# Sigmoid attention with a two-layer product after it: another order of loads, of partial products and of VectorE's sums

## The chip, the cores and the metric

The kernel runs on one core of one Trainium2 chip. The metric is the device time of one execution in microseconds (us). All runs quoted were at a granted TensorE clock of 0.997 to 1.0 wherever the record lists it. A span is the time from the first to the last instruction of the one execution that was profiled; it is 1.7 to 1.8 us shorter than the time of the same run.

PE is TensorE, DVE is VectorE, ACT is ScalarE, POOL is GpSimd (which issues the loads here) and SP is SyncE.

## The reference

```python
# q, k, v: (8, 12, 448, 64)   w_in: (768, 2048)   w_out: (2048, 768)
scores = matmul(q, k^T) / sqrt(64) - log(448)
attn   = matmul(1 / (1 + exp(-scores)), v)
x      = attn.transpose(0, 2, 1, 3).reshape(3584, 768)
h      = x @ w_in
out    = (h * cos(h)) @ w_out
```

## The kernel before

The kernel is written by a small scheduler. It keeps a model clock, keeps lists of what could be done next on each engine, and emits one instruction group at a time. What comes out is a fixed program: each engine runs its own queue in order and waits where its next instruction is not ready. The parameters at the head of the kernel steer only that order.

PE has these kinds of work. "T": transposes of early q and k. "S": scores. "AV": the sigmoid of the scores times v. "m1": the first product, `x @ w_in`. A **block**: 256 rows of the second product. The first block is plain. Each of the other 13 is made by a scheme with seven partial products instead of eight. A partial product is eight matmuls into one PSUM bank (the memory that TensorE writes its sums to), and VectorE then drains the bank, that is, copies or adds its contents to where they are needed.

```python
ORDER = [1, 6, 2, 7, 5, 4, 3]              # the seven products, in PE's order

def pe_prod(i, p, bk):                     # eight 128x384 matmuls into bank bk
    lhs, rhs, first, last = {
        1: (a11, b11, True, False),  2: (a12, b21, False, True),
        3: (s4, b22, False, True),   4: (a22, t4, False, True),
        5: (s1, t1, True, False),    6: (s2, t2, True, False),
        7: (a21, b12, False, False),
    }[p]
    ...
def dve_prod(p, bk, st, p1):               # the drain of that bank
    o = banks[bk][:, 0:HD]
    if p == 1:   nc.vector.tensor_copy(out=p1, in_=o)
    elif p == 2: nc.vector.tensor_copy(out=stages[st[0]], in_=o)
    elif p == 6: tt(stages[st[1]], o, p1, ALU.add)
    ...                                    # 7, 4 alike; 5 and 3 add to a stage
def gsum(eng, i, n, m, parts): ...         # s1, s2, a21 - .., s4: four sums per block
def dve_g(b, fp, part, hslot, cslot): ...  # h * cos(h), in pieces of 64 to 384 rows

def try_dve():                             # what VectorE gets next
    i = min(range(len(dve_q)), key=lambda n: (dve_q[n][0], n))   # priority, then age
    if DVE_PICK.get(dve_n[0], -1) < len(dve_q):
        i = DVE_PICK.get(dve_n[0], i)                            # or a set place
    ...
def try_pe():                              # what PE gets next
    kind = PE_PICK.get(order_at[0])        # a set kind at a set decision,
    ...                                    # otherwise S, T, AV, blocks, m1 by rules
for tok in LOADS.split():                  # the order of the first loads
    add_load(tok)
```

Two banks serve the blocks: products 1 and 2 fill one in turn, 6, 7 and 4 the other, and 5 and 3 take the first again. So PE may start a product only when VectorE has drained the product before the last. Besides its drains and sums VectorE copies the first product out of PSUM ("hs"), multiplies h by its cosine (line L355), and prepares q and k for the transposing DMA ("ri", L236).

Of the kernel before, what the change touches and what calls it, by code (L numbers as in the profile page):

```python
# [12 lines left out]
def kernel(  # L13
# [42 lines left out]
    N_RI = 2  # L56
    SIN_BURST = 3
    SIN_MIN = 1
    SIN_AT = [33]
    N_SIG0 = 4  # L60
    AV_MIN0 = 1
    AV_MIN = 6
# [2 lines left out]
    S_MAX2 = 2  # L65
    K_PIECE = 2
    M1_OPEN = 2
    M2_AT = [18, 10, 25, 58, 44, 52, 13, 44, 56, 62, 49, 48, 58, 64]
    M2_EAGER = True
    LOADS = 'y2 q1 x1 v0 x0 q2 v1 v3 q3 y0 x3 v2 q4 x2 b3 v4 b0 y1 y3 q5 q6 o0 b1 v8 v5 q7 v7 o1 b2 o3 v6 o2 q8'  # L70
    N_PLAIN = 1
    P_G = 2
    P_W = 2
    P_AV = 0
    P_IL = 1
    DUP_DVE = 4
    DUP_LEAD = 1.2
    P_DUP = 1
    T_LATE = 4
    T_AHEAD = 18  # L80
    HALF1 = 6
    HALF3 = 8
    HALF_MAX = 4
    W_POOL = False
    W_PIECES = 4
    G_POOL = ()
    PE_PICK = {28: 'm', 57: 't', 75: 'm', 539: 'm', 604: 'm'}
    DVE_PICK = {79: 2, 154: 1}
    WARM = 9
    WARM_END = 90.0  # L90
    TP_LAND = 9.0
    RAW_MARGIN = 3.0
    OUT_LAND = 4.0
# [134 lines left out]
    def dve_T(s, i, bk, j0, j1):  # L228
        dst = (kTs, qTs)[i][s % N_QKT]
        src = banks[bk].bitcast(fp16)[:, 0 : 2 * S].rearrange("p (x t) -> p x t", x=2)  # L230
        nc.vector.tensor_copy(out=dst[:, :, PT * j0 : PT * j1], in_=src[:, :, PT * j0 : PT * j1])
# [62 lines left out]
    def dve_dup(s, y):  # L294
        x = xts[s % N_X]
        nc.vector.tensor_copy(
            out=x[64 - 64 * y : 128 - 64 * y, 1], in_=x[64 * y : 64 * y + 64, 0]
        )
# [93 lines left out]
    def dve_wsum(n):  # L392
        b11, b12, b21, b22 = w_quarters()
        t1, t2, t4 = w_sum
        if n == 0:
            tt(t1, b12, b11, ALU.subtract)
        elif n == 1:
            tt(t2, b22, t1, ALU.subtract)
        elif n == 2:
            tt(b12, b22, b12, ALU.subtract)  # L400
        else:
            tt(t4, b21, t2, ALU.subtract)
# [180 lines left out]
    def add_load(tok):  # L583
        n = int(tok[1:])
        seen.add(tok)
        loads.extend(
            {
                "q": lambda: l_kq(n),
                "v": lambda: l_v(n),
                "a": lambda: l_wi(n, 0, 2),  # L590
                "b": lambda: l_wi(n, 2, 3),
                "x": lambda: l_wi(n, 0, 1),
                "y": lambda: l_wi(n, 1, 2),
                "w": lambda: l_wi(n),
                "o": lambda: l_wo(n),
            }[tok[0]]()
        )

    for tok in LOADS.split():
        add_load(tok)  # L600
# [16 lines left out]
    def wsums():  # L617
# [3 lines left out]
        for n in range(4):  # L621
            dve_q.append((P_W, 1.67, lambda n=n: dve_wsum(n), fin))

# [76 lines left out]
    def m1_job():  # L700
# [10 lines left out]
        b, fp = m1_next  # L711
        if b >= B or len(m1_open) >= M1_OPEN or len(m1_half) >= HALF_MAX:
            return None
# [91 lines left out]
    def start_av(s, js):  # L805
# [12 lines left out]
        def done():  # L818
# [12 lines left out]
            def fin():  # L831
# [6 lines left out]
                if s < DUP_DVE or ahead < DUP_LEAD:  # L838
                    for y in range(2):
                        dve_q.append((min(pri, P_DUP), 0.3, lambda y=y: dve_dup(s, y), dup_fin))  # L840
                else:
# [14 lines left out]
    def t_job():  # L856
# [3 lines left out]
        if (  # L860
            s_next[0] >= NJ * s - T_AHEAD
            and raw_got.get(s, 0) > (i if s else t_next[0])
# [6 lines left out]
    def start_t(s, i, j0, j1):  # L869
# [5 lines left out]
        def done():  # L875
# [3 lines left out]
            def fin():  # L879
# [6 lines left out]
            dve_q.append(  # L886
                (-2 if s_next[0] < SIN_AT[0] else 1, 0.065 + 0.067 * n, lambda: dve_T(s, i, bk, j0, j1), fin)
            )
# [182 lines left out]
    def try_pe():  # L1071
        if busy["pe"]:
            return
        kind = PE_PICK.get(order_at[0])
        order_at[0] += 1
# [16 lines left out]
    def heuristic():  # L1092
# [18 lines left out]
        jobs = NFP * m1_next[0] + m1_next[1]  # L1111
        want = not m1_open and quad_i[0] < NQUAD and jobs >= M2_AT[quad_i[0]]
        if j2 is not None and (want or (M2_EAGER and not m1)):
# [13 lines left out]
    def warm_up():  # L1127
        if clock[0] < WARM_END and s_next[0] < NJ * NSU:
            cur = av_cur.get(av_next[0])
            if any_bank():  # L1130
                pe_warm((single_free or pair_free)[0], 0, 128, ident)
            elif cur:
                pe_warm(cur["wd"], S, 512 - S, ident)
            else:
                return
            mode[0] = "full"
            run("pe", 0.055 if any_bank() else 0.03, lambda: None, 0.0)
# [35 lines left out]
    def try_act():  # L1173
# [12 lines left out]
        if not m2_on and len(hs_ready) >= SIN_BURST:  # L1186
            late = True
        if bursts[0] < len(SIN_AT) and sig_n[0] < SIN_AT[bursts[0]] and (act_q or hs_free or hs_extra) and table[0] == "sig":
            b_ok = False
# [37 lines left out]
    def try_dve():  # L1227
        if busy["dve"] or not dve_q:
            return
        i = min(range(len(dve_q)), key=lambda n: (dve_q[n][0], n))  # L1230
        if DVE_PICK.get(dve_n[0], -1) < len(dve_q):
            i = DVE_PICK.get(dve_n[0], i)
        dve_n[0] += 1
# [87 lines left out]
```

## Time and profile before

| | before |
|---|---|
| time, median of 4 runs | 382.24 us (380.77 to 382.8) |
| span of the profiled run | 379.6 us |
| PE, DVE, ACT busy | 97%, 77%, 69% |
| first 128x384 matmul | 83.0 us |
| last matmul ends | 375.3 us |

PE's busy time tells little here, because records of matmuls overlap. I use another measure throughout: the **time that PE lost** up to a moment. It is that moment less the sum of PE's useful work before it at its undisturbed pace: 0.189 us for a set of four 64x64 tiles of 448 columns, 0.1625 us for a 128x384 matmul, 0.0275 us for a transpose; small warm-up matmuls count as loss. These paces are the median distances between starts in undisturbed stretches of the trace before.

Of the profile before, the prediction below shows the tail. Here is the middle: the order of time in block 3, which took 10.4 us instead of 9.1. Columns: start, length, engine, line, operation, and in brackets how long the engine had idled and what ended that.

```profile
169.69 0.40 DVE L236 COPY ri<-qraw 128x896 f16<-128x896 f16 x1 [0.30 <-DMA qraw<-in_q_dram]
170.00 0.55 DVE L456 COPY p<-bk 128x384 f32<-128x384 f32 x1
170.47 1.15 DVE L355 TENSOR_TENSOR g_ring<-hs,cs 128x128 f16<-128x128 f32 x2
170.61 3.00 PE L426 MATMUL bk<-wo,g_ring 128*128 128x384 f16 x16 [0.43 <-DVE p L456]
171.54 0.55 DVE L365 TENSOR_TENSOR stage<-bk,p 128x384 f32<-128x384 f32 x1
172.00 1.15 DVE L355 TENSOR_TENSOR g_ring<-hs,cs 128x128 f16<-128x128 f32 x2
173.07 0.55 DVE L458 COPY stage<-bk 128x384 f32<-128x384 f32 x1
```

VectorE's queue is in order. A preparation that waited 0.30 us for a DMA stood ahead of the first drain (170.00), and PE, which needed that bank, started its third product 0.59 us late. After that come two cosine products (1.07 us) and a drain (0.47 us) for each product of PE. That is 1.54 us where PE needs 1.30.

### The profile page before, as it was taken

How to read it: one execution, taken by the hardware profiler on the slowest of the kernel's cores; microseconds unless marked ns; L12 is line 12 of the kernel's file. 1: busy time of each engine (PE TensorE's matmuls, PEld its weight loads, DVE VectorE, ACT ScalarE, POOL GpSimd, SP SyncE). 2: the span in 40 equal slices, each digit the busy share in tenths (PEclk: the TensorE clock that was granted, in tenths of full speed). 3: DMA queues.
4: the chain of work that ended last, by engine and by line, in shares of the span. 5: the costliest groups of instructions: out<-in, count | busy, mean ns of one | idle time of the engine just before them, and what ended most of it. 6: DMA issues, size and time to landing. Idle time of an engine off the chain costs nothing.

```text
span 379.6 us, 12680 instructions
## 1 busy us (share of the span) xinstructions
PE 369.2 (97%) x5563; PEld 232.7 (61%) x5563; DVE 292.9 (77%) x494; ACT 260.7 (69%) x266; POOL 69.5 (18%) x105
## 2 busy tenths in 40 slices
PE   8999999999999999999999999999999999999995
PEld 5666576665675775665665765565666566555553
DVE  2387889979999769569679597848586999868662
ACT  4989899996988896798796966574999744111000
POOL 8669531220311220220220202020000000000000
PEclk9999999999999999999999999999999999999999
DMA  9999999999999699599698947396411210133333
GB/s 160 201 197 199 203 212 206 149 130 130 119 161 127 136 121 161 86 157 123 95 157 155 114 83 127 77 120 150 82 26 26 54 35 2 32 71 67 85 83 83
DMA packets 70278, 44.60 MB, mean 117 GB/s; under 512 B 32592, under 2 KB 70224, under 8 KB 70224
## 3 DMA queue, kind: packets, MB, share of 16 engines
q0 software_dynamic: 30000, 22.49, 45.7%
q1 hardware_dynamic: 40144, 21.22, 31.6%
q8 instruction: 43, 0.70, 0.8%
q14 instruction: 11, 0.09, 0.1%
q10 hardware_dynamic: 80, 0.10, 0.1%
HBM read 45.61 MB, written 11.01 MB: 149 GB/s over the span
## 4 chain that ended last, share of the span: by engine, by line
PE 36%; DVE 11%; ACT 4%; issue 2%; DVEq 0%; ACTq 0%
PE bk L426 17%; PE pr L316 7%; PE bk L316 6%; DVE g_ring L355 5%; PE pr L277 3%; PE pr L251 3%; DVE hs L330 2%; ACT sig L260 2%; DVE stage L365 2%; ACT cs L333 1%; ACT L333 1%; DVE gs L390 1%; DVE g_ring L390 1%; DVE stage L458 0%; DVE xt L287 0%
## 5 line engine op out<-in xcount | busy, mean ns | idle before, releaser
L260 ACT ACTIVATE sig<-pr,lgs_t 128x896 f16<-128x896 f32 x159 | 148.6, 1011 | 41.1 <-PE pr L251 40.7
L316 PEld LDWEIGHTS <-wi 64*64 64x64 f16 x3072 | 99.7, 107 | 45.7 <-issue 3.2
L316 PE MATMUL pr<-xt,wi 64*64 64x448 f16 x2000 | 111.1, 349 | 0.4 <-DVE xt L287 0.2
L333 ACT ACTIVATE cs<-hs,pih_t 128x896 f16<-128x896 f32 x62 | 60.8, 1033 | 30.1 <-DVE hs L330 29.2
L355 DVE TENSOR_TENSOR g_ring<-hs,cs 128x768 f16<-128x768 f32 (+2 forms) x132 | 72.9, 589 | 1.4 <-ACT cs L333 1.1
L316 PE MATMUL bk<-xt,wi 64*64 64x448 f16 x1072 | 63.8, 349 | 0.3 <-DVE hs L330 0.2
L251 PE MATMUL pr<-qT,kT 64*64 64x448 f16 x672 | 61.0, 355 | 1.9 <-ACT sig L260 1.7
L426 PEld LDWEIGHTS <-g_ring 128*128 128x128 f16 x416 | 39.7, 98 | 33.1 <-issue 8.3
L330 DVE COPY hs<-pr 128x896 f32<-128x896 f32 x41 | 44.5, 1087 | 18.5 <-PE pr L316 16.2
L426 PE MATMUL bk<-wo,g_ring 128*128 128x384 f16 x312 | 55.7, 326 | 1.7 <-DVE stage L365 1.1
L184 POOL DMA_DIRECT2D vt<-in_v_dram x21 | 14.8, 706 | 178.7 <-PE pr L277 157.6
L426 PEld LDWEIGHTS <-gs 128*128 128x128 f16 x312 | 30.5, 98 | 21.1 <-issue 1.0
L426 PE MATMUL bk<-ws,gs 128*128 128x384 f16 x208 | 38.0, 326 | 0.1
L251 PEld LDWEIGHTS <-kT 64*64 64x64 f16 x672 | 26.1, 105 | 18.3 <-issue 6.8
L330 DVE COPY hs<-bk 128x448 f32<-128x448 f32 x42 | 24.2, 616 | 11.8 <-PE bk L316 11.6
L287 DVE CAST xt<-pr 128x896 f16<-128x896 f32 x19 | 20.7, 1089 | 14.5 <-PE pr L277 14.5
L277 PE MATMUL pr<-sig,vt 64*64 64x448 f16 x504 | 31.1, 350 | 0.0
L365 DVE TENSOR_TENSOR stage<-bk,p 128x384 f32<-128x384 f32 x39 | 21.6, 553 | 8.4 <-PE bk L426 8.4
L277 PEld LDWEIGHTS <-vt 64*64 64x64 f16 x588 | 18.9, 107 | 9.1 <-issue 1.3
L333 ACT ACT_TABLE_LOAD x16 | 20.5, 1283 | 5.1 <-DVE hs L330 4.8
L260 ACT ACT_TABLE_LOAD x15 | 19.2, 1283 | 5.7 <-PE pr L251 5.4
L426 PE MATMUL bk<-wo,gs 128*128 128x384 f16 x104 | 19.0, 326 | 0.3 <-DVE stage L365 0.2
(72 smaller groups left out, 285.3 us busy)
## 6 DMA issues: line engine op xcount, KB each, us to landing
out_dram<-stage SPq DMA_DIRECT2D x111, 96.0 KB, 2.2
vt<-in_v_dram POOLq DMA_DIRECT2D x21, 224.0 KB, 5.2
kraw<-in_k_dram POOLq DMA_DIRECT2D x19, 224.0 KB, 5.7
qraw<-in_q_dram POOLq DMA_DIRECT2D x19, 224.0 KB, 6.8
wi<-in_moe_w_in_dram POOLq DMA_DIRECT2D x24, 128.0 KB, 6.4
wo<-in_moe_w_out_dram POOLq DMA_DIRECT2D x4, 768.0 KB, 13.4
xt<-xt SPq DMA_DIRECT2D x24, 112.0 KB, 5.7
ws<-in_k_dram POOLq DMA_DIRECT2D x4, 224.0 KB, 7.4
```

What stands on the lines that cost most here:

```text
L184: nc.gpsimd.dma_start(out=vt_of(s), in_=v[b, 4 * g : 4 * g + 4].rearrange("(y x) (p j) d -> (x p) y (j d)", y=2, j=NJ),)
L251: nc.tensor.matmul(out=pairs[wd][64 * x : 64 * x + 64, y, 0:S], lhsT=kT[64 * y : 64 * y + 64, x, PT * j : PT * j + PT], rhs=qT[64 * y : 64 ...
L260: nc.scalar.activation(out=sgs[slot], in_=pairs[wd][:, :, 0:S], func=AF.Sigmoid, bias=lgs_t, scale=0.125,)
L277: nc.tensor.matmul(out=two(wd)[x][64 * y : 64 * y + 64, 0:S], lhsT=vt[64 * x : 64 * x + 64, y, D * j : D * j + D], rhs=sgs[slot][64 * x : ...
L287: nc.vector.tensor_copy(out=out, in_=pairs[wd][r0:r1, :, 0:S])
L316: nc.tensor.matmul(out=two(wd)[r][64 * m : 64 * m + 64, 0:S], lhsT=w_in_sb[c][64 * r : 64 * r + 64, h, 128 * f + 64 * m : 128 * f + 64 * m ...
L330: nc.vector.tensor_copy(out=out, in_=src)
L333: nc.scalar.activation(out=css[cslot], in_=hss[hslot], func=AF.Sin, bias=pih_t, scale=1.0)
L355: nc.vector.tensor_tensor(out=out.rearrange("p n e t -> p e n t"), in0=hss[hslot][:, :, t : t + w].rearrange("p e (n t) -> p e n t", t=min ...
L365: nc.vector.tensor_tensor(out=out, in0=in0, in1=in1, op=op)
L390: eng.tensor_tensor(out=out, in0=in0, in1=in1, op=op)
L426: nc.tensor.matmul(out=banks[bk][:, 0:HD], lhsT=lhs[:, kk, :], rhs=rhs[:, kk, :], start=first and kk == 0, stop=kk == HF - 1, skip_group_c ...
```

## The change

Only parameters of the scheduler change. The intent is the same work in an order in which PE waits less: another order of the loads of v and w_in, picks on PE (`'m'`: a piece of m1 ahead of scores), and picks and priorities that move sums and other pieces in VectorE's order.

```diff
-    SIN_AT = [33]
+    SIN_AT = [19]
-    M2_AT = [18, 10, 25, 58, 44, 52, 13, 44, 56, 62, 49, 48, 58, 64]
+    M2_AT = [26, 18, 27, 53, 53, 42, 27, 60, 52, 62, 53, 62, 59, 51]
-    LOADS = 'y2 q1 x1 v0 x0 q2 v1 v3 q3 y0 x3 v2 q4 x2 b3 v4 b0 y1 y3 q5 q6 o0 b1 v8 v5 q7 v7 o1 b2 o3 v6 o2 q8'
+    LOADS = 'y2 q1 x1 v0 x0 q2 v1 y0 q3 v4 b0 v3 v2 b3 q4 y1 x3 x2 q5 y3 q6 v8 o0 b1 v5 q7 o3 v7 b2 o1 v6 o2 q8'
-    P_W = 2
+    P_W = 1
-    P_DUP = 1
+    P_DUP = 0
-    T_AHEAD = 18
+    T_AHEAD = 7
-    HALF_MAX = 4
+    HALF_MAX = 3
-    PE_PICK = {28: 'm', 57: 't', 75: 'm', 539: 'm', 604: 'm'}
-    DVE_PICK = {79: 2, 154: 1}
+    PE_PICK = {28: 'm', 43: 's', 57: 't', 108: 'm', 116: 'm', 125: 'm', 208: 'a', 265: 'a', 299: 'm', 441: 'm', 539: 'm', 561: 'm'}
+    DVE_PICK = {54: 3, 57: 1, 76: 1, 79: 1, 82: 0, 148: 1, 224: 2, 431: 1, 471: 1, 482: 1}
-    WARM_END = 90.0
+    WARM_END = 160.0
```

## The prediction

> **What bounds the kernel now.** I read the page first, then the PE column in stretches, then the waits of PE and DVE, then the order of time where PE stands still. The head of the page (busy us, share of the span, instructions):
>
> ```profile
> PE 369.2 (97%) x5563; PEld 232.7 (61%) x5563; DVE 292.9 (77%) x494; ACT 260.7 (69%) x266; POOL 69.5 (18%) x105
> ```
>
> PE has work in flight in 97% of a span of 379.6 us. That number flatters, since records of pipelined matmuls overlap, so I also added the PE program up from starts of instructions. Four 64x448 matmuls of the attention and first product run as one set of four 64x64 tiles: 0.189 us a set. There are 672 for scores, 672 for the attention times v and 3072 for the first product, 4416 / 4 = 1104 sets, 208.7 us. The 64 + 728 matmuls of 128x384 start 0.1625 us apart: 128.7 us. 252 transposes at about 0.0275 us: 6.9 us. Nine warm-up matmuls at 0.43 us and 94 small ones at 0.056 us: 9.1 us. Sum: 353.4 us. The PE program has 72 changes between the 64x64, 128x64 and 128x128 shapes, each about 0.10 us more than a step within one shape (0.281 us against 0.180 from a 64x448 set to a 128x384 matmul): 7.2 us. The first matmul starts at 1.2 us and the last ends 4.2 us before the end. That makes 366 us; the other **13 to 14 us are stalls of PE**. They are all that an order alone can win, apart from the 5.3 us of small warm-up matmuls that stand in for waiting at the start.
>
> Where are they? Next comes the table of stretches for the line of the partial products (length of the stretch, then PE busy and count), one stretch for each of the 13 blocks that are made of seven products of eight matmuls:
>
> ```profile
> 114.50:123.60 9.10, 9.09 (x56) 5.40 (x56) 1.00 1.35 131
> 140.80:150.50 9.70, 9.47 (x56) 5.38 (x56) 1.00 1.03 165
> 167.40:177.80 10.40, 9.74 (x56) 5.37 (x56) 1.00 1.16 158
> 194.80:204.50 9.70, 9.40 (x56) 5.33 (x56) 1.00 1.10 174
> ```
>
> The first block runs clean: 56 x 0.1625 = 9.1 us. The third takes 10.4 us for the same 56 matmuls. Read so, with the gap ahead of each block counted, the excess over 9.1 us and over the shape change is 0.14 us (block 2, before it), 0.56 (2), 1.31 (3), 0.67 (4), 0.23 (7), 0.32 (8), 0.28 (9), 0.15 (10), 0.15 (11), and 0.61 before each of blocks 12 and 13, which follow their predecessor at once: about 5.0 us in all. The rest, roughly 5 to 6 us, lies before 70 us, in pieces of 0.2 to 0.7 us, and some 2 us are scattered. The order of time near the end shows what one such piece is made of:
>
> ```profile
> 353.47 0.56 DVE L365 TENSOR_TENSOR stage<-bk,stage 128x384 f32<-128x384 f32 x1 [0.74 <-PE bk L426]
> 353.94 0.68 DVE L390 TENSOR_TENSOR gs<-g_ring 128x1024 f16<-128x1024 f16 x1
> 354.57 1.46 PE L426 MATMUL bk<-wo,gs 128*128 128x384 f16 x8
> 354.66 0.69 DVE L390 TENSOR_TENSOR gs<-gs,g_ring 128x1024 f16<-128x1024 f16 x1
> 355.27 0.69 DVE L390 TENSOR_TENSOR g_ring<-g_ring 128x1024 f16<-128x1024 f16 x1
> 355.87 0.55 DVE L365 TENSOR_TENSOR stage<-bk,p 128x384 f32<-128x384 f32 x1
> 356.34 0.55 DVE L365 TENSOR_TENSOR stage<-bk,stage 128x384 f32<-128x384 f32 x1
> 356.48 1.46 PE L426 MATMUL bk<-wo,g_ring 128*128 128x384 f16 x8 [0.44 <-DVE stage L365]
> ```
>
> The product whose bank is drained at 355.87 had ended near 354.7, but VectorE first did three sums for the next block (0.68 us each). The next block needs that bank, so PE starts at 356.48 and not at 354.57 + 1.30 = 355.87: 0.61 us lost. The same stands at 366.18. In the middle of the kernel the three sums do no harm, since another stage of the work follows the block.
>
> **What the Trainium skill says.** (1) "Perfetto Trace Analysis", Identifying the Most-Contended Engine: matmul busy time is not a good measure of the distance to the bound, because pipelined instructions overlap. The trace agrees: one 128x384 matmul is recorded at 326 ns while two start 162.5 ns apart, which is why I count starts. (2) "TensorE: Matmul & The Clock Gate", Architectural detail: ScalarE and VectorE are strict FIFO queues, TensorE only pulls weight loads ahead. The trace agrees above: a drain that was ready stood 1.1 us behind sums. So VectorE's order is a cost by itself. (3) "TensorEngine Tiling (Array Packing)", Key Properties: a change of tiling mode drains the engine. The trace shows about 0.10 us for one. (4) "ScalarE: Activation LUTs", What ACT_TABLE_LOAD costs: 1283 ns for a load, plus a drain. The page has 1283 ns for each of 32 loads.
>
> **The change part by part.** I compared the program orders of both kernels by engine (no time is in them).
>
> *Work.* PE has the same matmuls but 98 small warm-up ones instead of 94: + 4 x 0.056 = +0.2 us. There are 75 changes of shape instead of 72: +0.3 us. ScalarE does the same 232 activations and 34 table loads instead of 32: 2 x 1.28 = 2.6 us of ScalarE, which is 69% busy and has nothing after about 345 us; on the path I count 0. VectorE drains the same banks; one first-product job drains in one piece of 1.09 us instead of two of 0.62, and two half-width copies of an x tile (0.435 us each) replace one DMA pair. Nothing that matters.
>
> *Last 70 us.* From the last attention work on, PE's order is the same in both (98 sets, a block, 12 sets, a block, 12 sets, three blocks). VectorE's is not: after blocks 11 and 12 it now goes sum, sum, drain, sum, drain instead of sum, sum, sum, drain, drain. With the durations above, the drain starts at 355.27 and ends by 355.8, so PE's next product can start about when the earlier one is through, 355.87. The third sum then ends at about 356.4 and the next drain at 356.9, before PE wants that second bank at 357.2. **Gain 2 x 0.6 = 1.2 us**, the surest term.
>
> *Blocks 2 to 8.* A product takes 1.30 us, its drain 0.47 (start to start), and PE writes to a bank again one product later, so VectorE may put about 1.30 - 0.47 - 0.2 = 0.6 us of other work ahead of each drain without holding PE. I summed the work ahead of the drains of each block, with a g piece at 0.26 us (128 wide) to 0.93 (768 wide) and a transpose preparation at 0.40. The largest lag behind 1.30 us per product, before the block's own sums come, is in before 1.1 (block 3), 1.2 (4), 0.9 (2), 0.65 (5 and 7), else under 0.5. In after it is 0.3 (3), 0.8 (4), 0.8 (2), 0.9 (5), 0.7 (7), else under 0.5. Measured stalls of before follow such lags less about 0.5 us, except block 3, where a preparation that waited 0.30 us for a DMA stood ahead of the first drain; in after both preparations stand behind that drain. Block 3 should win about 1 us, block 4 about 0.3, block 2 0.2, block 5 may lose 0.3, block 7 0.1 to 0.5. **Gain about 1.0 us**, give or take 1.
>
> *First 70 us.* The second third of one w_in slice comes ahead of a v and a q/k pair, another v is pulled forward, later w_in slices go back; first-product sets are picked ahead of scores at set places, and the transposes of later q and k are taken nearer to their use. DMA is the resource here: 198 to 209 GB/s in the four stretches from 20 to 60 us, about the highest in the page. The same bytes pass, so only what PE does while it waits can change. Of 5 to 6 us of stalls I give it 1 us, unsure: the picks look like answers to just these gaps, but the small warm-up matmuls of the new program move to a later place, which says that some gap is expected there too. **Gain about 0.8 us**, give or take 2.
>
> Sum: +0.2 + 0.3 - 1.2 - 1.0 - 0.8 = -2.5 us, from 381.7 to **379.2 us**, -0.7%.
>
> **The rivals.** (a) *The stall moves.* If the banks or ScalarE are the true limit before 70 us (ScalarE is 90 to 100% busy from 30 to 80 us, and PE's own wait for it is listed below), a new order changes which matmul waits and not how long. For: the few direct waits of PE are on ScalarE. Against: they add up to 1.7 us. Then only the tail and blocks gain: 380.0 us, or no gain at all if VectorE is late elsewhere.
>
> ```profile
> PE pr L251 <- ACT sig L260: 1.7, 5, 0.5
> PE bk L426 <- DVE stage L365: 1.3, 4, 0.4
> ```
>
> (b) *Loads come late.* A v or w_in slice that was moved back is not there when the new fixed order asks for it, and PE, which cannot go round it, stands. For: DMA is full there, landing takes 5 to 8 us. A single such wait would be 1 to 3 us: 381 to 384 us. (c) *The early gaps close in full.* Then up to 5 us come there and 2 in the blocks: 374 to 376 us. Against: ScalarE's near full load, and the need to fetch the first 10 MB at about 200 GB/s.
>
> **Range and chances.** The terms' doubts are about 2, 1 and 0.3 us, and the three runs of before spread over 2 us, so 80% is about 2.7 us to either side: 376.5 to 381.9. Faster by over 2% means under 374.1 us, 7.6 of some 13 us of stalls won: 0.04. Slower by over 2% (389.4) needs a long wait on a load, which a few reordered loads hardly make: 0.01. Within 2%: 0.95.
>
> **What would show it.** Right: blocks 12 and 13 start with no wait on the drain; block 3 takes under 9.6 us; PE's sum of starts grows by about 0.5 us from changes of shape and warm-up; PE's stalls before 70 us, from starts, shrink by 0 to 3 us. Wrong: if the tail shows no gain, the drain was not what held the bank; if the first 70 us end more than 2 us earlier or later, measured at the start of the first block of plain products (83.0 us in before), the load order was worth more than I gave it; if a block from 2 to 8 takes over 10.4 us, a lag that I counted small was not.

## The result, and the profile after

The changed kernel took 378.03 us (377.53 to 379.12, 4 runs) against 382.24 us. The ratio is 0.99, 95% interval 0.9862 to 0.9938. A ratio is the mean time of one kernel's fast runs over that of the other's fast runs of the same rounds, so it is not quite the ratio of the medians. The time predicted was 379.2 us with a range of 376.5 to 381.9: the result lies inside, a little faster than the point.

The span fell from 379.6 to 376.5 us. PE's useful work is the same in both. The time that PE lost, by stage, from the two traces:

| stage | before | after | gain |
|---|---|---|---|
| up to the plain block (83.0, 83.2 us) | 21.85 | 22.07 | -0.22 |
| from there to the start of block 5 | 4.57 | 2.41 | 2.16 |
| start of block 5 to start of block 11 | 3.20 | 3.16 | 0.04 |
| from there to the last matmul | 1.37 | 0.17 | 1.20 |

In this pair of traces nothing came from the first 83 us, about two thirds of the gain came from the stage of blocks 1 to 4, and the rest from the tail. Two of these figures hide something. The first 83 us hold a gain of about 0.5 us that a late start of this one execution covers; the experiments below show it. And the 0.04 us between blocks 5 and 11 is a sum of opposites: block 5 lost 0.25 us more, while the stretch between blocks 7 and 8, where a score waits for a sigmoid of ScalarE, lost 0.69 us instead of 0.98.

Here are the blocks in the table of stretches for the line of the partial products, first of the kernel after: blocks 1, 2, 3, 4, 5, 12 and 13 (the stretch, its length, then busy time and count of PE and of its weight loads, the granted clock, the busy share of DMA, and GB/s).

```profile
114.50:123.60 9.10, 9.09 (x56) 5.39 (x56) 1.00 1.11 179
140.60:149.90 9.30, 9.26 (x56) 5.37 (x56) 1.00 1.05 151
166.80:176.30 9.50, 9.37 (x56) 5.38 (x56) 1.00 0.97 121
193.30:202.50 9.20, 9.20 (x56) 5.35 (x56) 1.00 1.03 167
217.90:227.30 9.40, 9.30 (x56) 5.38 (x56) 1.00 0.53 83
353.90:363.00 9.10, 9.10 (x58) 5.47 (x57) 1.00 0.41 88
363.00:372.10 9.10, 9.10 (x57) 5.37 (x55) 1.00 0.40 86
```

And the last two blocks of the kernel before, each taken from the end of the block ahead of it:

```profile
355.90:365.60 9.70, 9.26 (x57) 5.47 (x56) 1.00 0.38 83
365.60:375.30 9.70, 9.26 (x57) 5.37 (x55) 1.00 0.37 81
```

56 matmuls at an undisturbed pace are 9.1 us. Block 3 went from 10.4 to 9.5 us, block 4 from 9.7 to 9.2, block 2 from 9.7 to 9.3, and blocks 12 and 13 from 9.7 to 9.1 each; block 5 lost 0.3. The order of time at the start of block 12 of the kernel after answers to the tail in the prediction:

```profile
352.67 0.69 DVE L390 TENSOR_TENSOR gs<-gs,g_ring 128x1024 f16<-128x1024 f16 x1
353.28 0.55 DVE L365 TENSOR_TENSOR stage<-bk,p 128x384 f32<-128x384 f32 x1
353.75 0.68 DVE L390 TENSOR_TENSOR g_ring<-g_ring 128x1024 f16<-128x1024 f16 x1
353.89 1.46 PE L426 MATMUL bk<-wo,g_ring 128*128 128x384 f16 x8
```

The drain now stands between the second and the third sum, and PE starts at 353.89 us with no wait: the product ahead of it had started at 352.58, and 352.58 + 1.30 = 353.88.

PE's own list of waits (engine and line, what it waited for: us in total, times, longest) loses the entries of the blocks and keeps the ones of the start and of the sigmoids. Of the kernel after, whole:

```profile
PE bk L219 <- DVE pih_t L1273: 1.2, 1, 1.2
PE pr L251 <- ACT sig L260: 1.0, 4, 0.3
PE pr L316 <- ACT sig L260: 0.2, 1, 0.2
```

### The profile page after: what moved, and what is told of

It is laid out like the page before. It is cut to its first block, busy times and chain, and to the rows that moved or that the text cites. A ratio compares the mean times of both kernels' runs of the same rounds, so it can differ in the third digit from the quotient of the medians.

```text
span 376.5 us, 12682 instructions
## 1 busy us (share of the span) xinstructions
PE 369.0 (98%) x5567; PEld 231.2 (61%) x5567; DVE 292.4 (78%) x496; ACT 264.0 (70%) x268; POOL 69.8 (19%) x105
## 4 chain that ended last, share of the span: by engine, by line
PE 50%; ACT 2%; issue 1%; DVE 1%; DVEq 0%; ACTq 0%
PE bk L426 23%; PE pr L316 14%; PE bk L316 5%; PE pr L277 3%; PE pr L251 3%; ACT sig L260 1%; DVE g_ring L355 0%; ACT L333 0%; DVE stage L365 0%; ACT cs L333 0%; DVE p L456 0%; DVE ri L236 0%; DVE stage L458 0%; DVE hs L330 0%; DVEq L236 0%
## 5 line engine op out<-in xcount | busy, mean ns | idle before, releaser
L316 PEld LDWEIGHTS <-wi 64*64 64x64 f16 x3072 | 98.1, 107 | 47.2 <-issue 3.3
L330 DVE COPY hs<-pr 128x896 f32<-128x896 f32 x42 | 45.5, 1086 | 12.8 <-PE pr L316 12.3
L287 DVE CAST xt<-pr 128x896 f16<-128x896 f32 x19 | 20.7, 1090 | 21.9 <-PE pr L277 21.8
L251 PEld LDWEIGHTS <-kT 64*64 64x64 f16 x672 | 24.9, 105 | 16.9 <-issue 5.7
L330 DVE COPY hs<-bk 128x448 f32<-128x448 f32 x40 | 23.1, 616 | 7.2 <-PE bk L316 7.1
L426 PE MATMUL bk<-ws,g_ring 128*128 128x384 f16 x104 | 19.0, 326 | 0.1
```

The costliest lines, as they stand in the source:

```text
L251: nc.tensor.matmul(out=pairs[wd][64 * x : 64 * x + 64, y, 0:S], lhsT=kT[64 * y : 64 * y + 64, x, PT * j : PT * j + PT], rhs=qT[64 * y : 64 ...
L287: nc.vector.tensor_copy(out=out, in_=pairs[wd][r0:r1, :, 0:S])
L316: nc.tensor.matmul(out=two(wd)[r][64 * m : 64 * m + 64, 0:S], lhsT=w_in_sb[c][64 * r : 64 * r + 64, h, 128 * f + 64 * m : 128 * f + 64 * m ...
L330: nc.vector.tensor_copy(out=out, in_=src)
L426: nc.tensor.matmul(out=banks[bk][:, 0:HD], lhsT=lhs[:, kk, :], rhs=rhs[:, kk, :], start=first and kk == 0, stop=kk == HF - 1, skip_group_c ...
```

## The experiments

My theory: the gain is the order of VectorE's queue, in blocks 2 to 4 and at the tail. The first rival: it is the new order on PE and of the loads, and VectorE's order only follows. The second: a wait in a block that is taken away by VectorE's order comes back later.

To change one engine's order and nothing else I let some kernels record what the scheduler emits, moved recorded operations, and emitted them then. All outputs are right.

The experiments were run in three calls, each on another chip and each with runs of the kernel before beside them (medians 381.64, 381.43 and 381.99 us). A comparison of two ratios of different calls, or of lost times, is also one of different chips.

Before and after are compared with the lost time as above. "Middle" means from the plain block to the start of block 11; "tail" means from there to the last matmul. "From first T" is the part of the time up to the plain block that was lost after PE's first transpose had started; PE has no useful work ahead of it.

| run | ratio to before (95%) | up to plain | from first T | middle | tail |
|---|---|---|---|---|---|
| before, first trace | 1 | 21.85 | 16.76 | 7.77 | 1.37 |
| after, first trace | 0.9900 (0.9862 to 0.9938) | 22.07 | 16.18 | 5.57 | 0.17 |
| after, again | 0.9904 (0.9886 to 0.9923) | 21.72 | 16.43 | 5.53 | 0.16 |
| after, sums first at the tail | 0.9940 (0.9922 to 0.9958) | 22.39 | 16.50 | 6.25 | 1.37 |
| before, drains ahead at the tail | 0.9969 (0.9951 to 0.9986) | 21.48 | 16.56 | 8.23 | 0.16 |
| before, VectorE's order in blocks 3, 4 | 0.9992 (0.9974 to 1.0009) | 22.09 | 17.15 | 6.94 | 1.37 |
| before, new loads | 1.0017 (0.9995 to 1.0039) | 21.55 | 16.51 | 7.73 | 1.37 |
| after, old loads | 0.9952 (0.9934 to 0.9969) | 23.67 | 17.86 | 5.53 | 0.16 |
| after, drains ahead in seven blocks | 0.9877 (0.9858 to 0.9896) | 21.30 | 16.19 | 5.03 | 0.01 |
| before, VectorE's order alone | 0.9916 (0.9899 to 0.9932) | 22.59 | 16.70 | 5.76 | 0.15 |
| after, drains ahead, block 9 too | 0.9865 (0.9849 to 0.9882) | 22.14 | 16.25 | 4.83 | 0.01 |

The tail is repeatable to 0.02 us. The time up to the plain block varies by a microsecond from run to run of one program: 21.3 to 22.4 us over the five traces that share the changed kernel's early program and loads, 21.5 to 22.6 over the four that share the old one's. The middle varies by half a microsecond or more where the program there is the same (5.53 to 6.25 us, and 7.73 to 8.23).

Most of the early spread arises before PE's first transpose, where all these programs do the same: nine large warm-up matmuls and seven small ones. Here are the small ones and the first transposes, in the first trace of before and in the run with VectorE's order alone, which has the same order on PE:

```profile
4.61 0.55 PE L219 MATMUL bk<-ident 128*128 128x128 f16 x7
5.09 0.58 PE L208 MATMUL bk<-ident,qraw 128*64 128x128 f16 x14
```

```profile
5.01 0.95 PE L219 MATMUL bk<-ident 128*128 128x128 f16 x7
5.89 0.58 PE L208 MATMUL bk<-ident,qraw 128*64 128x128 f16 x14
```

In each trace the warm-up matmuls start at first at about twice their later distance (0.43 us and then 0.22 for the large ones, 0.107 and then 0.056 for the small), and the moment of the switch differs from one execution to the next. So the first transpose starts anywhere from 4.92 to 5.89 us, in either program. The column "from first T" leaves this out. With its own loads the old program then loses 16.56 to 17.15 us (mean 16.79, four traces) and the new one 16.18 to 16.50 (mean 16.31, five traces): no overlap, and about 0.5 us less. The expectations below were written without this and take the early gain for nil.

### The changed kernel again

No edit; a control.

> The changed kernel, unaltered, as a control for the others of this call. Both theories: about 1.0% under before (378.0 against 382.2 us), span near 376.5 us, PE reaching the plain block at about 83.2 us against 83.0 us in before, so that nothing of the gain comes from the first 83 us. If the early part differs by more than 0.5 us from the first trace, the early part is noisier than I take it to be.

Measured: 377.88 us (377.38 to 379.18, 6 runs), ratio 0.9904. Plain block at 82.9 us. The early part differed by 0.35 us from the first trace, within the 0.5 I allowed. The gain of 1% is confirmed. Up to the plain block it again shows almost nothing early (21.72 against 21.85 us); from the first transpose it does (16.43 against 16.76).

### The changed kernel without its two last picks

```diff
-    DVE_PICK = {..., 224: 2, 431: 1, 471: 1, 482: 1}
+    DVE_PICK = {..., 224: 2, 431: 1}
```

> The changed kernel without its last two picks of VectorE's order: after blocks 11 and 12 three sums stand again ahead of the drain. Nothing else moves on any engine. Theory (the last block's bank was held back by a drain behind sums): the wait of about 0.6 us before blocks 12 and 13 comes back, the span grows by 1.2 us to about 377.7 us, and nothing before 344 us moves. Rival (the tail was won by something else, as the last attention work ending earlier): 0 us, under 0.3 us in any case.

Measured: 379.39 us, ratio 0.9940 against 0.9904, so 0.36% or 1.4 us slower. The tail lost 1.37 us instead of 0.16 or 0.17. Its span, 378.7 us, is longer than I expected, because the first 83 us and blocks 4 and 7 went slower in this trace, and no edit touches those; the profiled execution was the slowest of the six. The order of time at the start of block 12 is the old one:

```profile
354.29 0.69 DVE L390 TENSOR_TENSOR g_ring<-g_ring 128x1024 f16<-128x1024 f16 x1
354.89 0.55 DVE L365 TENSOR_TENSOR stage<-bk,p 128x384 f32<-128x384 f32 x1
355.36 0.55 DVE L365 TENSOR_TENSOR stage<-bk,stage 128x384 f32<-128x384 f32 x1
355.50 1.30 PE L426 MATMUL bk<-wo,g_ring 128*128 128x384 f16 x7 [0.44 <-DVE stage L365]
```

The third sum runs ahead of the drain, and PE starts its product 0.61 us late. The rival (0.3 us at most) falls.

### The kernel before with the tail alone

```diff
-    DVE_PICK = {79: 2, 154: 1}
+    DVE_PICK = {79: 2, 154: 1, 469: 1, 480: 1}
```

> The kernel before with the two drains of the tail put ahead of the third sum, and nothing else. Theory: blocks 12 and 13 start with no wait, the span falls by 1.2 us to about 378.4 us, the time by 0.3%. Rival (the gain at the tail needs the other parts of the change): under 0.4 us.

Measured: 380.73 us against 381.64, ratio 0.9969; the span was 378.4 us. The tail lost 0.16 us instead of 1.37. Two picks in VectorE's order, with every other engine untouched, are worth 0.3%.

### The kernel before with VectorE's order in blocks 3 and 4

```diff
 # block 3 on VectorE (p, r, o: drains; i: preparation; g: cosine product; S: sum)
-i p g g r g g o g g r i r S S S r r S
+p i r g g o g r g r S S S r g r g S i
 # block 4, from its first drain on
-p i g g r g o g g r i r S S S r r S
+p i g r g o g r g r S S S r r S g i
```

> The kernel before with VectorE's order altered in blocks 3 and 4 alone, after the pattern of the changed kernel (the preparation of the transpose behind the first drain, the products with the cosine spread between the drains, the last of them behind the sums). Theory (the gain of the middle is VectorE's order inside the blocks): the stalls in block 3 (1.31 us) and block 4 (0.67 us) fall to 0.4 us in all or less, the span falls by 1.4 to 1.7 us. Rival (the middle was won by the other places of blocks and scores on PE; the work that I put off holds up what follows): the blocks shorten, but PE waits after them, and the span falls by less than 0.6 us.

Measured: 380.84 us against 381.43, ratio 0.9992, an interval that includes 1. Both blocks did become clean; the table of stretches of this run, blocks 3 and 4:

```profile
167.60:176.70 9.10, 9.10 (x56) 5.39 (x56) 1.00 1.13 159
194.60:203.70 9.10, 9.10 (x56) 5.38 (x56) 1.00 1.15 180
```

But the lost time of the middle fell by 0.83 us against the first trace of before, and not by 1.98: more than half was given back. The order of time in this run, 5 us after block 3, shows where:

```profile
179.95 2.22 DVE L355 TENSOR_TENSOR g_ring<-hs,cs 128x128 f16<-128x128 f32 x4
...
182.09 1.08 DVE L330 COPY hs<-pr 128x896 f32<-128x896 f32 x1
...
183.23 0.57 PE L316 MATMUL pr<-xt,wi 64*64 64x448 f16 x8 [0.75 <-DVE hs L330]
```

The work that I had put off made VectorE late. The drain of the first product (line L330) stood behind four cosine products, and PE waited for that bank: 0.92 us lost by starts. Another 0.2 us of the same kind followed block 4. The theory's number fails here, and the second rival holds for this edit: the wait moved to the next drain in the queue.

### The two load orders, exchanged

Both kernels recorded; only the places of the loads refilled.

```diff
 # kernel before: load places 10 to 49
-q2 v1 v3 q3 y0 x3 v2 q4 x2 b3 v4 b0 y1 y3 q5 q6 o0 b1 v8 v5 o1 q7 v7 b2 o3 v6
+q2 v1 y0 q3 v4 b0 v3 v2 b3 q4 y1 x3 x2 q5 y3 q6 v8 o0 b1 v5 q7 o3 v7 b2 o1 v6
 # kernel after: the reverse
```

> The kernel before with its loads issued in the changed kernel's order and every other engine's order as it was. Theory (the early part is bound by bytes and ScalarE; the order of loads only has to suit PE's order): no gain; PE comes to the plain block at 83.0 us plus 0 to 1.5 us, where slices of w_in that now come later are wanted. Rival (the new load order is good by itself, and is hidden in the changed kernel by its other early changes): PE comes there at least 0.5 us earlier.

> The changed kernel with its loads issued in the old order and every other engine's order as it is. Theory (orders of loads and PE belong together, the early part gained nothing): PE comes to the plain block 0.5 to 4 us later than the 83.2 us of the changed kernel, because it asks for slices earlier than they now come; the gain after 83 us, 3.4 us, stays. Rival (the load order has no bearing): within 0.3 us of the changed kernel everywhere.

Measured: the kernel before with the new loads took 382.21 us against 381.43, ratio 1.0017 with an interval that includes 1, and lost 21.55 us before the plain block (at 82.7 us), in the range of its old loads (21.5 to 22.6). Its six times spread from 380.92 to 383.16 us, and the profile fell on one of the quick ones (380.98), so what the slow ones lose is not known. The changed kernel with the old loads took 379.68 us, ratio 0.9952 against 0.9904 for its own loads, and lost 23.67 us before the plain block (at 84.8 us), about 1.7 us more than the mean of the five traces with its own loads (21.9), or 1.55 us more from the first transpose. Its middle and tail are unchanged at 5.53 and 0.16. The largest single wait, in the order of time of that run:

```profile
54.26 0.58 PE L208 MATMUL pr<-ident,kraw 128*64 128x128 f16 x14 [0.80 <-DMA kraw<-in_k_dram]
```

A transpose of k stands on PE until its load lands. So the new load order gains nothing for the old program, and the new program on PE needs it. The loads and PE's early order belong together, and together they lose about 0.5 us less than the old pair from the first transpose on. Which of the early edits brings that, no run here separates.

### VectorE's order alone, in the kernel before

The kernel of blocks 3 and 4, with the drain of the first product moved ahead of the cosine products after block 3 and after block 4, and the two picks of the tail. PE, ScalarE, loads and transposing DMAs keep the old order.

```diff
 # VectorE after block 3 (h: drain of the first product)
-i g g g g h
+i h g g g g
 # after block 4
-i g g g h
+i g h g g
```

> The kernel before with VectorE's order alone altered: blocks 3 and 4 as in the run on these two blocks, the drain of the first product ahead of the products with the cosine after block 3 and after block 4 (in that run PE waited 0.92 us there for a drain that stood behind four such products), and the two drains of the tail ahead of the third sum. Loads, PE and ScalarE keep the old order. Theory (the whole gain is VectorE's order, and PE's new order is not needed for it): the wait after block 3 goes, the span falls by 2.7 to 3.2 us to about 376.6 us, ratio about 0.992. Rival (the middle needs PE's new order, which has room for the work put off): another wait takes its place, only the 1.2 us of the tail and the 0.8 us of the earlier run stay, ratio about 0.995 or more.

Measured: 378.83 us against 381.99, ratio 0.9916. The wait after block 3 is gone, and blocks 3 and 4 stay clean:

```profile
168.10:177.20 9.10, 9.10 (x56) 5.39 (x56) 1.00 1.17 159
194.20:203.30 9.10, 9.10 (x56) 5.35 (x56) 1.00 1.16 182
```

The middle lost 5.76 us, against 7.77 in the first trace of before and 5.57 in that of after, and the tail 0.15. The order of VectorE's queue at a few dozen places gives 0.84% of the 1% that the whole change gives. What is left, 0.12% or 0.5 us against the changed kernel's second run, is the size of the early gain, though the intervals of the two ratios overlap. The first rival falls for the middle and the tail: PE's new order is not needed there. Not shown is that the change itself wins its middle by VectorE's order alone. My order is not the changed kernel's, PE's order in the middle differs there too, and no run puts the old VectorE order of blocks 2 to 4 under the new PE order. It also shows what became of the gain in the run on blocks 3 and 4: the same two blocks, with one more drain put in front each time, keep it.

### Drains ahead in the changed kernel

The changed kernel, recorded. In blocks 2, 3, 5, 8, 10 and 11 pieces of cosine products, and in block 3 also two copies of x, are moved behind the drains that they held up. The edit for block 9 had no effect in the first of the two kernels, because the piece that mattered stood ahead of the block's first drain; the second kernel moves that too.

```diff
 # block 10 and 11 on VectorE
-p g g r o r r
+p g r g o r r
 # block 8
-p r g o g g r g r S S S
+p r o g r g g r g S S S
 # block 9, second kernel (h: drain of the first product)
-g h p g r g g o r r
+h p g r g o g r g r
```

> The changed kernel with VectorE's order altered in blocks 2, 3, 5, 8, 9, 10 and 11, so that at most about 0.6 us of other work stands ahead of a drain; everything else as it is. Theory (VectorE's order inside the blocks is a cost of PE by itself, and the work put off can be done later at no cost): the stalls left in these blocks, 0.20, 0.39, 0.26, 0.41, 0.20, 0.15 and 0.15 us, mostly go, the span falls by 1.3 to 1.8 us to about 375 us. Rival (the work put off is wanted right after the block, so that the stall moves there): the blocks get shorter and the span falls by less than 0.5 us or grows.

> The faster version of the changed kernel (drains ahead in blocks 2, 3, 5, 8, 10, 11) with block 9 treated as well, where a product with the cosine stood ahead of a drain of the first product and of the first drain of the block (0.19 us). Theory: block 9 takes 9.1 us, 0.2 us less in the span than that version, ratio to before about 0.987. Rival: the products put off hold up the first product after block 9, no gain.

Measured: 377.03 us (ratio 0.9877) and 376.94 us (ratio 0.9865), against 377.88 (0.9904) for the changed kernel in the first of the two calls. The intervals of the second version and of the changed kernel do not overlap. Blocks 2, 3, 8 and 9 of the second version:

```profile
140.60:149.70 9.10, 9.05 (x56) 5.40 (x56) 1.00 0.95 152
166.70:175.80 9.10, 9.07 (x56) 5.40 (x56) 1.00 0.90 128
286.60:295.70 9.10, 9.10 (x56) 5.37 (x56) 1.00 0.26 57
320.80:329.90 9.10, 9.10 (x56) 5.34 (x56) 1.00 0.16 35
```

The stalls in the treated blocks are gone, but again not all is kept. In the first version 1.56 us of stalls in the six treated blocks went, and the loss after the plain block fell by 0.7 us (5.74 to 5.04). In the second version PE stands for 0.44 us at 180.5 us, after block 3, where the list of waits has a score waiting for an hs drain, and for 0.30 us at 230.7 us, after block 5. My expectation of 1.3 to 1.8 us was too high. This is the fastest version found: some 5 us under the kernel before.

## Why the prediction was right or wrong

**The time and the range**: right. 379.2 us stood against 378.03, inside the range. The gain was forecast as 2.5 us and came to 3.7 to 3.8 by the ratios; nearly all of the difference is in one term, blocks 2 to 8. By lost time it is 0.5 us early, 2.2 in the middle and 1.2 at the tail. The span of the first pair fell by only 3.1 us because the first transpose of that one execution started 0.8 us later (5.89 against 5.09).

**The bound**: right. PE's stalls were what changed, apart from a few warm-up matmuls and changes of shape, and the useful work of PE was the same. PE busy went from 97% to 98%, which told as little as the prediction said. Two readings in it were a little off, and no term of the gain rests on them: seven of the nine large warm-up matmuls of that trace took 0.43 us and two 0.22, and ScalarE was 84% busy from 40 to 50 us, not 90 to 100%.

**The tail** (a gain of 1.2 us): right, 1.37 to 0.17 us lost, and shown in both directions by the runs that undo it and that do it alone. The runs' times agree: 1.4 and 1.2 us.

**Blocks 2 to 8** (a gain of 1.0 us, give or take 1): the mechanism was right, the term too small. The middle gained 2.2 us. By blocks the prediction had 0.2, 1.0 and 0.3 us for blocks 2, 3 and 4; the stalls fell by 0.50, 0.92 and 0.59 us. Block 5 lost 0.25 us, as foretold (0.3). Block 7, where I feared a loss of 0.1 to 0.5 us, went from 0.24 to 0.18. The step that failed is the conversion of the largest lag on VectorE into a stall of PE, "less about 0.5 us". Block 3 of the changed kernel was counted with a lag of 0.3 us, so without a stall, and lost 0.40 us; block 5 of the kernel before was counted with 0.65 and lost 0.02. And one part of the middle is not a drain at all: the wait for a sigmoid between blocks 7 and 8, 0.29 us less lost, for which the prediction had no term.

**The first 70 us** (a gain of 0.8 us, give or take 2): about right in size. Up to the plain block nothing is seen (22.0 against 21.9 us in the mean of four and five traces), because of the varying start. From the first transpose on, the change gains about 0.5 us, in which the 0.5 us predicted for warm-ups and changes of shape are already paid; so the stalls there fell by about 1 us, as an estimate from these figures. Why is open. The prediction's reason, that "the picks look like answers to just these gaps", was not tested by itself. The exchange of load orders shows only that the new PE order needs the new loads, and that these gain no time for the old PE order.

**Changes of shape and warm-ups** (a cost of 0.5 us): the counts are as predicted, 75 changes instead of 72 and 98 small warm-up matmuls instead of 94. Their cost is inside the early part's loss and was not measured by itself.

**Rival (a), the stall moves**: not in the change itself, whose stalls in the middle and at the tail went for good. But it was real in my own edit of blocks 3 and 4, of whose 1.98 us more than half came back behind the next drain. **Rival (b), loads come late**: shown for the wrong pairing of loads and PE order, about 1.7 us, and which the change avoids. **Rival (c), the early gaps close in full**: no, about 1 us of them by the estimate above.

What stays open: what holds PE back in the first 83 us, where either program loses 22 us. As an estimate from the paces above, 15 us of these are the start (1.2), the warm-up matmuls (some 9) and 49 to 52 changes of shape (some 5), and about 7 are waits. ScalarE was busy for 73 of these 83 us in both traces, and DMA ran at 184 to 185 GB/s, but no run here took either away.

## What to carry to other kernels

When the bounding engine is 97% busy and the work is fixed, add up the starts of its instructions and list the gaps. In the blocks here, each gap of 0.2 to 0.6 us was a PSUM bank whose drain stood behind other work in an in-order queue, so put drains ahead of work that nobody waits for yet. Follow the work that you put off: it is still in the same queue, and the next drain behind it may be the one that PE waits for. And before you call a stage unchanged, look at where its spread from run to run arises: here 1 us of it came from the first 6 us, and a gain of 0.5 us stood behind it.

## What the Trainium skill lacked or had wrong

- "Perfetto Trace Analysis", Identifying the Most-Contended Engine: right that matmul busy time misleads (97% against 98% for a change of 1%). One of the two measures that it gives in its place, the busy share of weight loads, did not tell the kernels apart either: 61% in both. Summing starts against the undisturbed pace did, to 0.02 us at the tail.
- "TensorE: Matmul & The Clock Gate", Back-to-back issue gap: its sustained figure for pairs of weight load and matmul, about 131 ns at 512 columns, was not seen. Pairs of 384 columns started 162.5 ns apart, and sets of 448 columns 0.189 us apart. Both are the page's formula for the isolated matmul, columns / 2.4 + 2.5 ns (162.5 and 189.2).
- "TensorEngine Tiling (Array Packing)", Key Properties: says that a change of mode drains the engine, without a figure. Here a change cost about 0.10 us (0.281 us against 0.180 between starts).
- No page that I read has the cost of a drain's place in VectorE's queue: 0.61 us of PE for one drain behind one sum too many, 0.92 us for one behind four cosine products.
